# Query and key projections of a linear-attention kernel, one head at a time in the upper and lower 64 rows of the array

## The chip, the cores and the metric

The kernel runs on one core of a Trainium2 chip. The metric is the device time of one execution in microseconds; the time of a version is the median of its runs. TensorE is called PE here, VectorE DVE, ScalarE ACT, GpSimd POOL, and the queue from which transfers are issued SP.

## What is computed

Linear attention with exponential features over 4 batches, 8 heads, 576 tokens and 64 dimensions, then two feed-forward blocks over the 2304 tokens. The part that the change touches is `phi`:

```python
def phi(x):
    proj = np.einsum('bhsd,df->bhsf', x, w_phi)          # w_phi: 64 x 128
    proj = proj - np.max(np.abs(proj), axis=-1, keepdims=True)
    return np.concatenate([np.exp(proj), np.exp(-proj)], axis=-1)
q_p, k_p = (phi(q), phi(k))
kv = np.einsum('bhsf,bhsd->bhfd', k_p, v)
z = np.sum(k_p, axis=2)
num = np.einsum('bhsf,bhfd->bhsd', q_p, kv)
den = np.einsum('bhsf,bhf->bhs', q_p, z)[..., None] + 1e-06
x = num / den
```

The first feed-forward block is 512 to 2048 to 512 with a leaky rectifier; the second has four experts, each 512 to 1024 to 512, whose results are added with the weights of a table of probabilities. All inputs and outputs are float32.

## The kernel before

**Two stages.** The first stage does the attention for 16 pairs of heads (4 batches, 4 pairs each) and, as filler, the first group of four chunks of the first feed-forward block for three blocks of tokens. The second stage is a plain loop over the rest of the feed-forward work (`up` and `down`, lines 211 and 240).

**Precision.** Where float32 products are wanted at the rate of float32r, an operand is split into a rounded part and a rest (names ending in h and l), and three products are added: high by high, high by low, low by high.

**A pair of heads.** The two heads' 64 dimensions lie in the partitions 0 to 63 and 64 to 127 of `kh`, `kl`, `qh`, `ql`. The 576 tokens are cut into four tiles of 128 and one of 64 (`TILES`). `project` (line 339) multiplies a tile of tokens, loaded into the array as weights, by `wbh` and `wbl`: matrices of 128 rows and 256 columns that hold `w_phi` twice, upper left for the one head and lower right for the other, with zeros elsewhere. The result of a tile is 128 tokens by 2 x 128 features in a bank of PSUM. Units of work (`UNITS`, line 36) are two tiles, two tiles, and the tile of 64 tokens: 512, 512 and 256 columns. Per unit DVE finds the largest magnitude of each group of 128 columns (`largest`, line 352, instruction line 355) and subtracts it (`less`, line 358, instruction line 362); for keys ACT takes the exponentials of both signs (`exp_keys`, line 364, instruction line 368). `key_values` (line 372) then adds, per unit, the products of the exponentials with the values (line 379, two heads in two halves of the array's columns) and with ones (line 385, four column quarters). When the three units are through, the sums are copied (`save_kv`), transposed (`turn_kv`, lines 399 and 401) and copied again. For the queries `turn_queries` (line 412) transposes the differences of a head, 256 or 320 tokens at a time (`HALVES`), ACT takes exponentials, and `attend` (line 429) multiplies them by the transposed sums; `invert` and `x_part` divide.

**What sets the order.** The first stage is described as operations with costs per engine, predecessors, a rank and buffers (`op`, line 64). A planner (`Plan.run`, line 69) plays them through and emits each one when its turn comes: of the operations that are ready and have room in their rings it takes the one that can begin first, ties by rank. So the costs that the operations state decide the order of each engine's instructions. Rings limit how far it runs ahead: `bank` has five PSUM banks, which projections, transposes and attention products share; `pmk` two, `pmq` three, `ke` two, `gh` and `gl` five each, `t` two buffers. The operations are named P (project), R (largest), S (less), E (exponentials of keys), KV, CV, TV, T, X, A for attention, W for the words of the first weights, and U, G0, G1, G2, M for the feed-forward filler (PSUM tiles `mm`). A line such as

```python
op(("P", *key), {"t": pe(256, 3) * len(UNITS[u])}, [(n, "l", p)], pr_, alloc=[("bank", key), ("pm" + n, (p, u))],
```

says: PE works for three products of 256 columns per tile, after the split of that tensor, and claims a bank and a buffer for the differences.

Of the kernel before, what the change touches and what calls it, by code (L numbers as in the profile page):

```python
# [11 lines left out]
F32 = mybir.dt.float32  # L12
F32R = mybir.dt.float32r
# [6 lines left out]
P = 128  # L20
B, H, S, D, F = 4, 8, 576, 64, 128
# [5 lines left out]
E, DE = 4, 1024  # L27
# [4 lines left out]
BLK = 512  # L32
BLOCKS = [(t, min(BLK, NT - t)) for t in range(0, NT, BLK)]
NB = len(BLOCKS)
TILES = [(t * P, min(P, S - t * P)) for t in range(-(-S // P))]
UNITS = [(0, 1), (2, 3), (4,)]
HALVES = [(0, 256), (256, 320)]
HMAX = 320
NA = 3
AHEAD = 2  # L40
# [90 lines left out]
def fused(ctx: ExitStack, tc: tile.TileContext, qT, kT, v_main, v_tail, w_phi, alpha, probs, w64, wcat, out):  # L131
    nc = tc.nc
# [145 lines left out]
    with ExitStack() as st1:  # L278
# [8 lines left out]
        for args in (  # L287
            ("kr", 1, F32, P, S), ("qr", 1, F32, P, S), ("v", 1, F32, P, len(TILES), 2, D),
            ("kh", 1, F32R, P, S), ("kl", 1, F32R, P, S), ("qh", 1, F32R, P, S), ("ql", 1, F32R, P, S),
            ("m", 13, F32, P, 4), ("pmk", 2, F32, P, 4, F), ("pmq", 3, F32, P, 4, F), ("ke", 2, F32, P, 4, 2, F),  # L290
            ("kvs", 1, F32, P, 4, F), ("qe", 4, F32, P, 2, HMAX), ("kvt", 4, F32, P, 4, P),
            ("den", 2, F32, P, S), ("dt", 1, F32, P, S), ("num", 2, F32, P, S), ("di", 3, F32, P, S // 32, 1),
            ("gh", 5, F32R, P, BLK), ("gl", 5, F32R, P, BLK), ("t", 2, F32, P, BLK),
        ):
            ring(*args)
        ring("bank", 5, F32, P, 512, space=PSUM)
# [4 lines left out]
        tl = {}  # L301
# [35 lines left out]
                nc.sync.dma_start(new(n + "r", p), (qT if n == "q" else kT)[b, j])  # L337

        def project(p, n, u):
            xh, xl = tl[n + "h", (p,)], tl[n + "l", (p,)]  # L340
            unit = UNITS[u]
            rows = TILES[unit[0]][1]
            ps = new("bank", (n, p, u)).rearrange("p (m f) -> p m f", f=F)
            new("pm" + n, (p, u))
            for i, tile_ in enumerate(unit):
                o = ps[:rows, 2 * i:2 * i + 2, :]
                tok = slice(TILES[tile_][0], TILES[tile_][0] + rows)
                nc.tensor.matmul(o, xh[:, tok], wbh, start=True, stop=False)  # L348
                nc.tensor.matmul(o, xh[:, tok], wbl, start=False, stop=False)  # L349
                nc.tensor.matmul(o, xl[:, tok], wbh, start=False, stop=True)  # L350

        def largest(p, n, u):
            m, rows = 2 * len(UNITS[u]), TILES[UNITS[u][0]][1]
            ps = tl["bank", (n, p, u)].rearrange("p (m f) -> p m f", f=F)
            nc.vector.tensor_reduce(  # L355
                new("m", (n, p, u))[:rows, :m], ps[:rows, :m], AX.X, ALU.max, apply_absolute_value=True)

        def less(p, n, u):
            m, rows = 2 * len(UNITS[u]), TILES[UNITS[u][0]][1]
            ps = tl["bank", (n, p, u)].rearrange("p (m f) -> p m f", f=F)  # L360
            mx = tl["m", (n, p, u)][:rows, :m, None].to_broadcast([rows, m, F])
            nc.vector.tensor_tensor(tl["pm" + n, (p, u)][:rows, :m], ps[:rows, :m], mx, ALU.subtract)  # L362

        def exp_keys(p, u):
            m, rows = 2 * len(UNITS[u]), TILES[UNITS[u][0]][1]
            e = new("ke", (p, u))
            for s, sc in ((0, 1.0), (1, -1.0)):
                nc.scalar.activation(e[:rows, :m, s], tl["pmk", (p, u)][:rows, :m], AF.Exp, scale=sc)

        flat = lambda x: x.rearrange("p i s f -> p i (s f)")  # L370

        def key_values(p, u):

            unit = UNITS[u]
            rows, e, v = TILES[unit[0]][1], flat(tl["ke", (p, u)]), tl["v", p]
            kv = new("kv", p) if u == 0 else tl["kv", p]
            for i, tile_ in enumerate(unit):
                for h in range(2):
                    nc.tensor.matmul(  # L379
                        kv[h * D:(h + 1) * D, 0], v[:rows, tile_, h], e[:rows, 2 * i + h],  # L380
                        start=tile_ == 0, stop=tile_ == len(TILES) - 1, skip_group_check=True)
            for i, tile_ in enumerate(unit):
                for h in range(2):
                    r = 32 * (2 * (tile_ % 2) + h)
                    nc.tensor.matmul(  # L385
                        kv[r:r + 32, 1], ones[:rows], e[:rows, 2 * i + h],
                        start=False, stop=tile_ + 2 >= len(TILES), tile_position=(0, r), skip_group_check=True)

        def save_kv(p, k, e):
            kvs = (new if k == 0 else lambda *x: tl[x])("kvs", p).rearrange("p (k s) f -> p k (s f)", k=2)  # L390
# [21 lines left out]
        def turn_queries(p, h, c):  # L412
            c0, n = HALVES[c]
            ps = new("bank", ("t", p, h, c))
            new("qe", (p, h, c))
            for u, unit in enumerate(UNITS):
                for i, tile_ in enumerate(unit):
                    t0, rows = TILES[tile_]
                    if c0 <= t0 < c0 + n:
                        nc.tensor.transpose(  # L420
                            ps[:, t0 - c0:t0 - c0 + rows], tl["pmq", (p, u)][:rows, 2 * i + h], ident[:rows, :rows])

        def exp_queries(p, h, c):
            n = HALVES[c][1]
# [41 lines left out]
        for p in range(len(pairs)):  # L466
            for n in "kq":
                op(("ld", n, p), {"d": 900}, [], RANK["ld"] + p, alloc=[(n + "r", p)], late=2000,
                   emit=lambda e, p=p, n=n: load(p, n))
                two(n, (p,), n + "r", p, S, [("ld", n, p)], RANK["sp"] + p)  # L470
                for u in range(3):
                    key = (n, p, u)
                    pr_ = RANK["P" + n] + p + 0.1 * u
                    op(("P", *key), {"t": pe(256, 3) * len(UNITS[u])}, [(n, "l", p)], pr_, alloc=[("bank", key), ("pm" + n, (p, u))],
                       behind=[("A", p - AHEAD, 1, 1)] * (p >= AHEAD),
                       reads=[(n + "h", (p,)), (n + "l", (p,))], emit=lambda e, a=(p, n, u): project(*a))
                    op(("R", *key), {"v": dve(N_U[u])}, [("P", *key)], pr_, alloc=[("m", key)],
                       emit=lambda e, a=(p, n, u): largest(*a))
                    op(("S", *key), {"v": dve(N_U[u])}, [("R", *key)], pr_,
                       reads=[("bank", key), ("m", key)], emit=lambda e, a=(p, n, u): less(*a))  # L480
            op(("ld", "v", p), {"d": 900}, [], RANK["ld"] + p, alloc=[("v", p)], late=2000, emit=lambda e, p=p: load(p, "v"))
            for u in range(3):
                op(("E", p, u), {"a": 2 * act(N_U[u])}, [("S", "k", p, u)], RANK["E"] + p + 0.1 * u, alloc=[("ke", (p, u))],
                   reads=[("pmk", (p, u))], emit=lambda e, a=(p, u): exp_keys(*a))
            for u in range(3):
                op(("KV", p, u), {"t": 595 * len(UNITS[u])}, [("E", p, u), ("ld", "v", p)] + [("KV", p, u - 1)] * (u > 0),
                   RANK["KV"] + p + 0.1 * u, alloc=[("kv", p)] if u == 0 else [], reads=[("ke", (p, u)), ("v", p)],
                   emit=lambda e, a=(p, u): key_values(*a))
            for k in range(2):
                op(("CV", p, k), copy_cost(256), [("KV", p, 2)], RANK["TV"] + p, alloc=[("kvs", p)] if k == 0 else [],  # L490
                   behind=[("CV", p, 0)] * k, reads=[("kv", p)], emit=lambda e, a=(p, k): save_kv(*a, e))
            op(("TV", p), {"t": 340}, [("CV", p, 0), ("CV", p, 1)], RANK["TV"] + p, alloc=[("bank", ("kv", p)), ("kvt", p)],
               reads=[("kvs", p)], emit=lambda e, p=p: turn_kv(p))
# [4 lines left out]
            for c in range(2):  # L498
                for h in range(2):
                    key, n = (p, h, c), HALVES[c][1]  # L500
                    pr_ = RANK["Q"] + p + 0.2 * c + 0.1 * h
                    us = ((0,), (1, 2))[c]
                    op(("T", *key), {"t": 110 * len(us) + 110 * (1 - c) + 50 * c}, [("S", "q", p, u) for u in us], pr_,
                       alloc=[("bank", ("t", *key)), ("qe", key)], reads=[("pmq", (p, u)) for u in us], emit=lambda e, a=key: turn_queries(*a))
                    op(("X", *key), {"a": 2 * actp(n)}, [("T", *key)], pr_,
                       reads=[("bank", ("t", *key))], emit=lambda e, a=key: exp_queries(*a))
                    pr_ = RANK["A"] + p + 0.2 * c + 0.1 * h
                    op(("A", *key), {"t": pe(4 * n, 2)}, [("X", *key), *kv_done], pr_, reads=[("qe", key), ("kvt", p)], behind=[("A", p, 0, 0)] * (h + c > 0),
                       alloc=[("bank", ("n", *key))] + [("den", p), ("num", p)] * (h == c == 0),
                       emit=lambda e, a=key: attend(*a))  # L510
                    op(("D", *key), copy_cost(n), [("A", *key)], pr_,
                       reads=[("bank", ("n", *key))], emit=lambda e, a=key: take(*a, "den", e))
                    op(("N", *key), copy_cost(n), [("A", *key)], pr_,
                       reads=[("bank", ("n", *key))], emit=lambda e, a=key: take(*a, "num", e))
# [191 lines left out]
```

## Time and profile before

| | us |
|---|---|
| median of 3 runs | 1438.12 (1437.93 to 1438.18) |
| the profiled execution, device time | 1439.93 |
| its span on the core | 1438.2 |
| PE busy, share of the span | 1418.9, 99% |
| DVE busy | 654.7, 46% |
| ACT busy | 412.4, 29% |
| POOL busy | 212.4, 15% |

The first stage takes roughly the first 300 us. Busy time is the union of the instructions' recorded times; ends of matmuls are modelled, so starts are the better measure, and the distance from one start to the next is called the pace below. PEld is the loading of weights into the array, which overlaps products. A float32 product that is not a transpose appears in the trace as two products and two loads.

### The profile page before, as it was taken

Reading aid. Unit: us, or ns where it says so; the run is one execution under the profiler, and the core shown is the slowest. Engines: PE = TensorE matmul, PEld = TensorE weight load, DVE = VectorE, ACT = ScalarE, POOL = GpSimd, SP = SyncE. Lnnn points to the kernel's source line nnn. Section 1 sums busy time; section 2 is a strip of 40 time slices with the busy share of each in tenths; the row PEclk is TensorE's granted clock in tenths of the full one; section 3 lists DMA queues with packets and bytes.
Section 4 is the critical chain, followed back from the end, with each engine's and each line's share of the span. In section 5 each row is a group of like instructions: output and inputs, shape, how many; then the busy total and the mean of one; then the engine's idle time right before and its main releaser. Section 6 shows DMA issues by size and latency. Waiting matters only on the chain.

```text
span 1438.2 us, 17632 instructions
## 1 busy us (share of the span) xinstructions
PE 1418.9 (99%) x7200; PEld 1152.1 (80%) x7200; DVE 654.7 (46%) x1067; ACT 412.4 (29%) x857; POOL 212.4 (15%) x165
## 2 busy tenths in 40 slices
PE   7999999999999999999999999999999999999998
PEld 4667667778888888888888888888888888888887
DVE  7966656687958855663222222222222222222222
ACT  6877666632212112232021120121210201211110
POOL 3443223102002002011020020020100200200100
PEclk9999999999999999999999999999999999999999
DMA  4311111130202001001020020010100200100001
GB/s 148 112 50 51 50 50 51 53 103 30 88 1 59 30 8 52 1 23 37 0 59 0 1 59 0 8 52 1 30 30 0 59 0 8 52 0 0 30 30 74
DMA packets 25136, 53.67 MB, mean 37 GB/s; under 512 B 3168, under 2 KB 4320, under 8 KB 25056
## 3 DMA queue, kind: packets, MB, share of 16 engines
q1 hardware_dynamic: 25056, 52.55, 12.2%
q8 instruction: 57, 0.93, 0.3%
q14 instruction: 23, 0.19, 0.0%
HBM read 47.82 MB, written 4.72 MB: 37 GB/s over the span
## 4 chain that ended last, share of the span: by engine, by line
PE 94%; DVE 3%; ACT 1%; DMA 1%; issue 0%; SPq 0%; POOL 0%; ACTq 0%; DVEq 0%; POOLq 0%
PE up L208 39%; PE dn L234 39%; PE bank L437 4%; PE kv L379 3%; PE mm L208 2%; PE kv L385 2%; PE mm L234 2%; PE bank L420 1%; PE bank L348 1%; PE bank L349 1%; PE bank L350 1%; DMA st<-w 1%; DMA acc_a<-w 0%; PE bank L401 0%; DVE m L355 0%
## 5 line engine op out<-in xcount | busy, mean ns | idle before, releaser
L208 PE MATMUL up<-Xl,whu 128*128 128x512 f32 (+1 forms) x912 | 334.6, 367 | 0.0
L208 PE MATMUL up<-Xh,whu 128*128 128x512 f32 (+1 forms) x912 | 334.5, 367 | 0.0
L208 PE MATMUL up<-Xh,wlu 128*128 128x512 f32 (+1 forms) x912 | 334.4, 367 | 0.0
L219 ACT ACTIVATE gh<-up 128x512 fp32r<-128x512 f32 (+1 forms) x160 | 88.7, 555 | 539.5 <-PE up L208 539.4
L220 DVE SCALAR_TENSOR_TENSOR gl<-up,gh 128x512 fp32r<-128x512 f32 (+1 forms) x160 | 102.0, 638 | 303.8 <-ACT gh L219 303.7
L234 PE MATMUL dn<-whd,gh 128*128 128x512 f32 x576 | 224.2, 389 | 0.0
L234 PE MATMUL dn<-wld,gh 128*128 128x512 f32 x576 | 224.2, 389 | 0.0
L234 PE MATMUL dn<-whd,gl 128*128 128x512 f32 x576 | 224.1, 389 | 0.0
L208 PEld LDWEIGHTS up<-Xh,whu 128*128 128x128 f32 x912 | 172.0, 189 | 28.6
L208 PEld LDWEIGHTS up<-Xl,whu 128*128 128x128 f32 x912 | 172.0, 189 | 28.4
L208 PEld LDWEIGHTS up<-Xh,wlu 128*128 128x128 f32 x912 | 171.9, 189 | 28.2
L161 POOL TENSOR_TENSOR wlu<-w,whu 128x512 fp32r<-128x512 f32 x44 | 58.2, 1322 | 915.3 <-ACT whu L158 879.7
L234 PEld LDWEIGHTS dn<-whd,gl 128*128 128x128 f32 x576 | 108.1, 188 | 22.5
L234 PEld LDWEIGHTS dn<-whd,gh 128*128 128x128 f32 x576 | 108.2, 188 | 22.1
L234 PEld LDWEIGHTS dn<-wld,gh 128*128 128x128 f32 x576 | 108.2, 188 | 22.1
L271 DVE SCALAR_TENSOR_TENSOR acc_a<-dn,pr,acc_a 128x512 f32<-128x512 f32 x72 | 50.2, 751 | 135.4 <-PE dn L234 135.4
L234 PE MATMUL dn<-gh,wld 128*128 128x512 f32 (+1 forms) x272 | 99.1, 364 | 0.0
L234 PE MATMUL dn<-gh,whd 128*128 128x512 f32 (+1 forms) x272 | 99.1, 364 | 0.0
L234 PE MATMUL dn<-gl,whd 128*128 128x512 f32 (+1 forms) x272 | 99.0, 364 | 0.0
L158 ACT CAST gh<-t 128x512 fp32r<-128x512 f32 (+1 forms) x68 | 38.6, 569 | 134.8 <-DVE t L224 134.6
L437 PE MATMUL bank<-qe,kvt 128*128 128x256 f32 (+1 forms) x256 | 72.6, 417 | 0.9 <-DVE pmk L362 0.9
L158 ACT CAST whu<-w 128x512 fp32r<-128x512 f32 x44 | 27.3, 620 | 136.4 <-PE up L208 121.4
(121 smaller groups left out, 1734.8 us busy)
## 6 DMA issues: line engine op xcount, KB each, us to landing
w<-wcat SPq DMA_DIRECT2D x64, 256.0 KB, 2.6
st<-w SPq DMA_DIRECT2D x24, 512.0 KB, 3.5
kr<-kT SPq DMA_DIRECT2D x16, 288.0 KB, 2.8
qr<-qT SPq DMA_DIRECT2D x16, 288.0 KB, 2.8
out<-o SPq DMA_DIRECT2D x18, 256.0 KB, 2.0
v<-v_main SPq DMA_DIRECT2D x16, 256.0 KB, 3.0
acc_a<-w SPq DMA_DIRECT2D x8, 512.0 KB, 4.5
v<-v_tail SPq DMA_DIRECT2D x16, 32.0 KB, 2.9
```

What stands on the lines that cost most here:

```text
L158: nc.scalar.copy(hi, src)
L161: lo_eng.tensor_tensor(lo, src, f32(hi), ALU.subtract)
L208: nc.tensor.matmul(ps[:, :bn], a[:, cs], x[:, cc, t0:t0 + bn], start=n == 0, stop=n == 3 * CC - 1)
L219: nc.scalar.activation(gh, ps, AF.Relu)
L220: nc.vector.scalar_tensor_tensor(gl, ps, 0.0, f32(gh), ALU.max, ALU.subtract)
L234: nc.tensor.matmul(ps, a, b, start=start and k == 0, stop=stop and k == 2)
L271: nc.vector.scalar_tensor_tensor(av, ps, pe, av, ALU.mult, ALU.add)
L348: nc.tensor.matmul(o, xh[:, tok], wbh, start=True, stop=False)
L349: nc.tensor.matmul(o, xh[:, tok], wbl, start=False, stop=False)
L379: nc.tensor.matmul(kv[h * D:(h + 1) * D, 0], v[:rows, tile_, h], e[:rows, 2 * i + h], start=tile_ == 0, stop=tile_ == len(TILES) - 1, skip ...
L385: nc.tensor.matmul(kv[r:r + 32, 1], ones[:rows], e[:rows, 2 * i + h], start=False, stop=tile_ + 2 >= len(TILES), tile_position=(0, r), ski ...
L437: nc.tensor.matmul(nd[:, :n], tl["kvt", p][:, 2 * h + s], tl["qe", (p, h, c)][:, s, :n], start=s == 0, stop=s == 1)
```

## The change

The units of work become the four full tiles of the first head, the four full tiles of the second head, and the tile of 64 tokens of both. The first two are projected in one operation: for each tile and each of the three terms one product per head, its tokens and `w_phi` from that head's 64 partitions, its 128 columns into that head's own bank. The last tile is projected as before. The maxima, subtractions and exponentials work on units of the same sizes as before, each now of one head. The products of keys and values are emitted for the four full tiles at once, after the exponentials of both heads, and then for the last tile: two operations in place of three. A transpose of the queries' first half waits for its own head's unit alone. The planner is told 12 products of 128 columns as the cost of the 24. The ring of `ke` grows from two to three; `gl` shrinks from five to four and `t` from two to one.

```diff
-UNITS = [(0, 1), (2, 3), (4,)]
+UNITS = [[(0, t) for t in range(4)], [(1, t) for t in range(4)], [(0, 4), (1, 4)]]
+UNIT_OF = {ht: (u, i) for u, unit in enumerate(UNITS) for i, ht in enumerate(unit)}
...
-            ("m", 13, F32, P, 4), ("pmk", 2, F32, P, 4, F), ("pmq", 3, F32, P, 4, F), ("ke", 2, F32, P, 4, 2, F),
+            ("m", 13, F32, P, 4), ("pmk", 2, F32, P, 4, F), ("pmq", 3, F32, P, 4, F), ("ke", 3, F32, P, 4, 2, F),
...
-            ("gh", 5, F32R, P, BLK), ("gl", 5, F32R, P, BLK), ("t", 2, F32, P, BLK),
+            ("gh", 5, F32R, P, BLK), ("gl", 4, F32R, P, BLK), ("t", 1, F32, P, BLK),
...
         def project(p, n, u):
...
-            for i, tile_ in enumerate(unit):
-                o = ps[:rows, 2 * i:2 * i + 2, :]
-                tok = slice(TILES[tile_][0], TILES[tile_][0] + rows)
-                nc.tensor.matmul(o, xh[:, tok], wbh, start=True, stop=False)
-                nc.tensor.matmul(o, xh[:, tok], wbl, start=False, stop=False)
-                nc.tensor.matmul(o, xl[:, tok], wbh, start=False, stop=True)
+            terms = ((xh, wbh), (xh, wbl), (xl, wbh))
+            us = (0, 1) if u == 0 else (2,)
+            ps = [new("bank", (n, p, v)).rearrange("p (m f) -> p m f", f=F) for v in us]
+            for v in us:
+                new("pm" + n, (p, v))
+            if u == 0:
+                for t in range(4):
+                    t0, rows = TILES[t]
+                    for k, (x, w) in enumerate(terms):
+                        for h in range(2):
+                            hs = slice(h * D, (h + 1) * D)
+                            nc.tensor.matmul(ps[h][:rows, t], x[hs, t0:t0 + rows], w[hs, h], start=k == 0, stop=k == 2)
+            else:
+                t0, rows = TILES[4]
+                for k, (x, w) in enumerate(terms):
+                    nc.tensor.matmul(ps[0][:rows, :2], x[:, t0:t0 + rows], w, start=k == 0, stop=k == 2)
...
+        def key_values(p, n):
+
+            ts = range(4) if n == 0 else (4,)
...
+                for u in (0, 2):
+                    key = (n, p, u)
+                    us = (0, 1) if u == 0 else (2,)
+                    op(("P", *key), {"t": pe(128, 12) if u == 0 else pe(256, 3)}, [(n, "l", p)], RANK["P" + n] + p + 0.1 * u,
+                       alloc=[(r, k) for v in us for r, k in (("bank", (n, p, v)), ("pm" + n, (p, v)))],
...
+            for n in range(2):
+                op(("KV", p, n), {"t": 595 * (4, 1)[n]}, [("E", p, u) for u in ((0, 1), (2,))[n]] + [("KV", p, 0) if n else ("ld", "v", p)],
...
-                    us = ((0,), (1, 2))[c]
-                    op(("T", *key), {"t": 110 * len(us) + 110 * (1 - c) + 50 * c}, [("S", "q", p, u) for u in us], pr_,
+                    us = ((h,), (h, 2))[c]
+                    op(("T", *key), {"t": 220 + 50 * c}, [("S", "q", p, u) for u in us], pr_,
```

The order of the instructions moves with it. In the lines below the part after the arrow names what is read and the part before it what is written; the size is that of the result.

On PE, before, the projection of the third pair's keys: its products of 256 columns come in pieces of two tiles, between transposes of the second pair (`pmq` are the queries' differences, `kvs` the sums of keys and values).

```order
L349 MATMUL bank<-wbl,kh 128x256
L350 MATMUL bank<-wbh,kl 128x256
L420 MATMUL bank<-ident,pmq 128x128 x2
L420 MATMUL bank<-ident,pmq 128x64
L399 MATMUL bank<-ident,kvs 128x128 x2
L401 MATMUL bank<-sel,kvs 128x64 x2
L348 MATMUL bank<-wbh,kh 128x256
L349 MATMUL bank<-wbl,kh 128x256
```

The same place in the change:

```order
L413 MATMUL bank<-sel,kvs 128x64 x2
L447 MATMUL bank<-qe,kvt 128x320 x2
L431 MATMUL bank<-ident,pmq 128x128 x2
L431 MATMUL bank<-ident,pmq 128x64
L355 MATMUL bank<-wbh,kh 128x128 x2
L355 MATMUL bank<-wbl,kh 128x128 x2
L355 MATMUL bank<-wbh,kl 128x128 x2
```

Three products of 256 columns have become three times two of 128, and the block of all four tiles stands behind the transposes instead of around them.

On PE, before, the products of keys and values of the second pair (`ke` are the keys' exponentials):

```order
L379 MATMUL kv<-ke,v 64x256 x4
L385 MATMUL kv<-ke,ones 32x256 x4
L420 MATMUL bank<-ident,pmq 128x128 x2
L379 MATMUL kv<-ke,v 64x256 x4
L385 MATMUL kv<-ke,ones 32x256 x4
L348 MATMUL bank<-wbh,kh 64x256
L349 MATMUL bank<-wbl,kh 64x256
```

And in the change:

```order
L359 MATMUL bank<-wbh,ql 64x256
L391 MATMUL kv<-ke,v 64x256 x8
L397 MATMUL kv<-ke,ones 32x256 x8
L447 MATMUL bank<-qe,kvt 128x256 x2
L391 MATMUL kv<-ke,v 64x256 x2
L397 MATMUL kv<-ke,ones 32x256 x2
```

Two blocks of four and four have become one of eight and eight, which stands behind all projections of the pair.

On DVE, before, the first pair's keys, whose exponentials the key products wait for (`acc_a` is the space in which words of weights are put together):

```order
L355 TENSOR_REDUCE m<-bank 128x4
L362 TENSOR_TENSOR pmk<-bank,m 128x512
L168 TENSOR_SCALAR acc_a<-acc_a 128x512
L169 SCALAR_TENSOR_TENSOR acc_a<-acc_a 128x512
L170 TENSOR_SCALAR acc_a<-acc_a 128x512
L171 SCALAR_TENSOR_TENSOR acc_a<-acc_a 128x512
L355 TENSOR_REDUCE m<-bank 128x4 x2
```

And in the change:

```order
L327 TENSOR_TENSOR ql<-qr,qh 128x576
L364 TENSOR_REDUCE m<-bank 128x4 x2
L371 TENSOR_TENSOR pmk<-bank,m 128x512 x2
L364 TENSOR_REDUCE m<-bank 128x4 x2
L371 TENSOR_TENSOR pmq<-bank,m 128x512
```

The maxima and subtractions of two units now follow each other, and the words of the weights come later.

## Rows read from the trace of the kernel before

**Rows 1.** The page: engines' busy time; the chain that ended last, by engine.

```profile
PE 1418.9 (99%) x7200; PEld 1152.1 (80%) x7200; DVE 654.7 (46%) x1067; ACT 412.4 (29%) x857; POOL 212.4 (15%) x165
...
PE 94%; DVE 3%; ACT 1%; DMA 1%; issue 0%; SPq 0%; POOL 0%; ACTq 0%; DVEq 0%; POOLq 0%
```

**Rows 2.** Busy time by stretch: length, PE, PEld, DVE, ACT, POOL, clock, DMA.

```profile
0.00:50.00 50.00, 40.04 (x270) 26.25 (x270) 40.29 (x67) 34.91 (x81) 20.67 (x23) 0.97 0.43 136
50.00:100.00 50.00, 47.12 (x319) 31.98 (x318) 37.69 (x64) 38.66 (x94) 23.22 (x17) 1.00 0.24 75
100.00:250.00 150.00, 150.00 (x1000) 105.50 (x999) 90.68 (x168) 104.48 (x253) 45.30 (x33) 1.00 0.18 52
```

**Rows 3.** Waits of PE over the span: us in total, times, longest us.

```profile
PE kv L379 <- ACT ke L368: 6.0, 6, 2.3
...
PE mm L208 <- DVE t L565: 2.7, 2, 1.7
PE bank L437 <- DVE pmk L362: 0.9, 3, 0.4
PE bank L420 <- DVE pmq L362: 0.8, 1, 0.8
```

**Rows 4.** The chain that ended last, in order of time: start, us, what.

```profile
52.16 0.70 DVE acc_a L171
...
60.85 0.63 ACT ke L368
...
61.52 1.08 PE kv L379 x8
...
93.55 2.75 PE mm L208 x12
```

**Rows 5.** PE in order of time, a projection: start us, us, line, form.

```profile
103.05 0.28 PE L348 MATMUL bank<-wbh,kh 128*128 128x256 f32 x1
...
104.00 0.28 PE L350 MATMUL bank<-wbh,kl 128*128 128x256 f32 x1
```

**Rows 6.** Instructions by line and form: one of the six groups of full projections.

```profile
L348 PE MATMUL bank<-wbh,kh 128*128 128x256 f32 x64 | 22.5, 352 | 4.7 <-ACT wbh L158 4.7
```

**Rows 7.** Loads of weights (PEld) in order of time, at two places.

```profile
102.58 0.19 PEld L348 LDWEIGHTS bank<-wbh,kh 128*128 128x128 f32 x1 [0.41 <-DVE di L450]
102.69 0.19 PEld L349 LDWEIGHTS bank<-wbl,kh 128*128 128x128 f32 x1
...
106.97 0.52 PEld L401 LDWEIGHTS bank<-sel,kvs 128*128 128x128 f32 x4
107.41 0.19 PEld L348 LDWEIGHTS bank<-wbh,qh 128*128 128x128 f32 x1
```

**Rows 8.** Loads by line and form (busy us, mean ns): transposes of 128 and 64 rows.

```profile
L420 PEld LDWEIGHTS bank<-ident,pmq 128*128 128x128 f32 x128 | 15.2, 144 | 9.6 <-issue 3.7 <-POOL wlu L548 1.1 <-DVE pmq L362 0.4
...
L420 PEld LDWEIGHTS bank<-ident,pmq 64*128 64x128 f32 x32 | 4.3, 135 | 5.3 <-issue 5.2 <-DVE acc_a L168 0.2
```

**Rows 9.** PE in order of time: into column tiles and back, and full float32 products.

```profile
108.12 0.28 PE L350 MATMUL bank<-wbh,ql 128*128 128x256 f32 x1
108.33 1.08 PE L379 MATMUL kv<-ke,v 128*64 128x256 f32 x8
109.34 0.64 PE L385 MATMUL kv<-ke,ones 128*32 128x256 f32 x8
109.91 0.33 PE L348 MATMUL bank<-wbh,kh 128*64 128x256 f32 x1
110.08 0.28 PE L349 MATMUL bank<-wbl,kh 128*64 128x256 f32 x1
...
116.13 2.10 PE L437 MATMUL bank<-qe,kvt 128*128 128x256 f32 x8
118.07 0.49 PE L420 MATMUL bank<-ident,pmq 128*128 128x128 f32 x3
```

**Rows 10.** Instructions of DVE and ACT by line and form: busy us, mean ns.

```profile
L355 DVE TENSOR_REDUCE m<-bank 128x4 f32<-128x512 f32 x64 | 41.5, 674 | 2.5 <-PE bank L350 2.3
...
L368 ACT ACTIVATE ke<-pmk 128x512 f32<-128x512 f32 x64 | 36.0, 622 | 1.5 <-DVE pmk L362 1.4
...
L362 DVE TENSOR_TENSOR pmk<-bank,m 128x512 f32<-128x512 f32 x32 | 20.6, 675 | 0.0
```

More of the change, by code (lines that the diff above doesn't have):

```diff
@@ L340, in project @@
             xh, xl = tl[n + "h", (p,)], tl[n + "l", (p,)]
[L341 to L344, printed above, removed]
-            for i, tile_ in enumerate(unit):
-                o = ps[:rows, 2 * i:2 * i + 2, :]
-                tok = slice(TILES[tile_][0], TILES[tile_][0] + rows)
-                nc.tensor.matmul(o, xh[:, tok], wbh, start=True, stop=False)
-                nc.tensor.matmul(o, xh[:, tok], wbl, start=False, stop=False)
-                nc.tensor.matmul(o, xl[:, tok], wbh, start=False, stop=True)
+            terms = ((xh, wbh), (xh, wbl), (xl, wbh))
[14 more added lines that the diff above has]
+                    nc.tensor.matmul(ps[0][:rows, :2], x[:, t0:t0 + rows], w, start=k == 0, stop=k == 2)
         def largest(p, n, u):
-            m, rows = 2 * len(UNITS[u]), TILES[UNITS[u][0]][1]
+            m, rows = len(UNITS[u]), TILES[UNITS[u][0][1]][1]
             ps = tl["bank", (n, p, u)].rearrange("p (m f) -> p m f", f=F)
@@ L358, in less @@
         def less(p, n, u):
-            m, rows = 2 * len(UNITS[u]), TILES[UNITS[u][0]][1]
+            m, rows = len(UNITS[u]), TILES[UNITS[u][0][1]][1]
             ps = tl["bank", (n, p, u)].rearrange("p (m f) -> p m f", f=F)
@@ L364, in exp_keys @@
         def exp_keys(p, u):
-            m, rows = 2 * len(UNITS[u]), TILES[UNITS[u][0]][1]
+            m, rows = len(UNITS[u]), TILES[UNITS[u][0][1]][1]
             e = new("ke", (p, u))
@@ L368, in exp_keys, with keys @@
                 nc.scalar.activation(e[:rows, :m, s], tl["pmk", (p, u)][:rows, :m], AF.Exp, scale=sc)
[L370 to L377, printed above, removed]
+        def key_values(p, n):
+            ts = range(4) if n == 0 else (4,)
+            v = tl["v", p]
+            kv = new("kv", p) if n == 0 else tl["kv", p]
+            def keys(h, t):
+                u, i = UNIT_OF[h, t]
+                return tl["ke", (p, u)].rearrange("p i s f -> p i (s f)")[:TILES[t][1], i]
+            for t in ts:
                 for h in range(2):
                     nc.tensor.matmul(
-                        kv[h * D:(h + 1) * D, 0], v[:rows, tile_, h], e[:rows, 2 * i + h],
-                        start=tile_ == 0, stop=tile_ == len(TILES) - 1, skip_group_check=True)
-            for i, tile_ in enumerate(unit):
+                        kv[h * D:(h + 1) * D, 0], v[:TILES[t][1], t, h], keys(h, t),
+                        start=t == 0, stop=t == len(TILES) - 1, skip_group_check=True)
+            for t in ts:
                 for h in range(2):
-                    r = 32 * (2 * (tile_ % 2) + h)
+                    r = 32 * (2 * (t % 2) + h)
                     nc.tensor.matmul(
-                        kv[r:r + 32, 1], ones[:rows], e[:rows, 2 * i + h],
-                        start=False, stop=tile_ + 2 >= len(TILES), tile_position=(0, r), skip_group_check=True)
+                        kv[r:r + 32, 1], ones[:TILES[t][1]], keys(h, t),
+                        start=False, stop=t + 2 >= len(TILES), tile_position=(0, r), skip_group_check=True)
         def save_kv(p, k, e):
@@ L415, in turn_queries @@
             new("qe", (p, h, c))
[L416 to L421, printed above, removed]
+            for t, (t0, rows) in enumerate(TILES):
+                if c0 <= t0 < c0 + n:
+                    u, i = UNIT_OF[h, t]
+                    nc.tensor.transpose(ps[:, t0 - c0:t0 - c0 + rows], tl["pmq", (p, u)][:rows, i], ident[:rows, :rows])
         def exp_queries(p, h, c):
@@ L470, in fused @@
                 two(n, (p,), n + "r", p, S, [("ld", n, p)], RANK["sp"] + p)
+                for u in (0, 2):
[3 more added lines that the diff above has]
+                       alloc=[(r, k) for v in us for r, k in (("bank", (n, p, v)), ("pm" + n, (p, v)))],
+                       behind=[("A", p - AHEAD, 1, 1)] * (p >= AHEAD),
+                       reads=[(n + "h", (p,)), (n + "l", (p,))], emit=lambda e, a=(p, n, u): project(*a))
                 for u in range(3):
@@ L473, in fused @@
                     pr_ = RANK["P" + n] + p + 0.1 * u
[L474 to L477, printed above, removed]
+                    op(("R", *key), {"v": dve(N_U[u])}, [("P", n, p, u - u % 2)], pr_, alloc=[("m", key)],
                        emit=lambda e, a=(p, n, u): largest(*a))
@@ L484, in fused @@
                    reads=[("pmk", (p, u))], emit=lambda e, a=(p, u): exp_keys(*a))
[L485 to L488, printed above, removed]
+            for n in range(2):
+                op(("KV", p, n), {"t": 595 * (4, 1)[n]}, [("E", p, u) for u in ((0, 1), (2,))[n]] + [("KV", p, 0) if n else ("ld", "v", p)],
+                   RANK["KV"] + p + 0.1 * n, alloc=[("kv", p)] if n == 0 else [],
+                   reads=[("v", p)] + [("ke", (p, u)) for u in ((0, 1), (2,))[n]], emit=lambda e, a=(p, n): key_values(*a))
             for k in range(2):
-                op(("CV", p, k), copy_cost(256), [("KV", p, 2)], RANK["TV"] + p, alloc=[("kvs", p)] if k == 0 else [],
+                op(("CV", p, k), copy_cost(256), [("KV", p, 1)], RANK["TV"] + p, alloc=[("kvs", p)] if k == 0 else [],
                    behind=[("CV", p, 0)] * k, reads=[("kv", p)], emit=lambda e, a=(p, k): save_kv(*a, e))
```

## Prediction

> **What bounds the kernel now.** I read the page first: TensorE (PE) is busy 99% of the span, and the chain of work that ended last lies 94% on PE [rows 1]. So PE's time is the kernel's time, unless a stretch shows otherwise. The table by stretch of time shows where it does: PE is idle for 9.96 us in the first 50 us, for 2.88 in the next 50, and not at all from 100 to 250 us [rows 2]; the granted clock is full there. The list of waits says for what: six waits of the key products (kv) for the exponentials of the keys (ke), 6.0 us in all, and small ones for VectorE (DVE) [rows 3]. Last the chain in order of time: at 52 us it still runs through DVE's words of the feed-forward weights and ScalarE's exponentials, and it turns to PE only at 61.5 us, with the kv product that had waited for ke [rows 4]. The reader should see two regimes: in the first 60 us a microsecond saved on PE becomes a wait, behind that it counts in full, and new waits count everywhere.
>
> **What the change does to the projections.** Per pair of heads and tensor, four tiles of 128 tokens each took three products over 256 columns: 384 in all (six groups like the one row shown, 64 each [rows 6]), and eight follow each other in 0.95 us, 0.119 us each [rows 5]. They become 384 couples: one product in the upper 64 rows of the array, one in the lower, 128 columns each. At the 0.119 us of 256 columns, 128 would stream in half of that, 0.06 us.
>
> But each of the 768 products loads its own tokens as weights, 128 columns of them, where one load served both heads. Two views price a load. After a pause, where nothing hides it, the second load starts 0.11 us behind the first; and where the products are only 64 columns long, four loads take 0.44 us, again 0.11 each [rows 7]. Half the rows do not halve it: the transposes' loads are recorded at 144 ns with 128 rows, at 135 ns with 64 [rows 8]. So if the two loads of a couple run side by side, the couple is bound by its loads, at 0.11 us, not by its columns: 384 × (0.119 − 0.11) = 3.5 us saved instead of 22.7.
>
> Do they run side by side? No row of the kernel before has two products in different rows of the array. In different columns it has: eight kv products of 256 columns start within 1.01 us, while eight full ones of the same length take 1.94 [rows 9], so two column halves work at once, loads included. I take the same for rows. The bounds of a couple are 0.06 us (columns alone) and 0.22 us (two loads in turn); I take 0.11, between them, since it is the load that rows 7 measure.
>
> The Trainium skill says otherwise of the gain: in "TensorE: Matmul & The Clock Gate", Part 3, products packed in different row groups take about the time of one of them plus some 4 ns for each further one. By that a couple would cost one short product, and this term would be −22.7 us instead of −3.5. The page's own rule on loads, that their time goes by columns and not by rows (Part 2), pulls the other way; rows 7 and 8 agree with it.
>
> **Changes of the array's shape.** Going from a full product to a column-tiled one takes 0.21 us from start to start instead of 0.12, and the first product behind a change is late by its load: 0.17 instead of 0.12 for 64 columns [rows 9]. That is 0.09 and 0.05 to 0.11, about 0.15 us for a change of shape. Along PE's order I count 202 changes before (products of float32r taken as using all columns, since rows 9 show no step between 128- and 64-column ones of them) and 187 in the change: the kv block of each pair is entered twice instead of three times, and the row-tiled blocks are entered 15 times from another shape, the others standing behind a 64-row transpose. 15 fewer × 0.15 = −2.2 us; the 15 entries load 128 columns uncovered, 0.05 more each, +0.8. Sum −1.4 us, between −2.2 and +2.
>
> **New waits.** Maxima, subtractions and exponentials stay the same in number and size (4 × 128 columns per unit, as before), so DVE and ScalarE do no more work. What moves is when a kv block may start. It now takes four tiles of both heads, so both first units must be through. From the end of the projections that is two maxima and two subtractions in a row on DVE, 4 × 0.675 us, then two exponentials, 2 × 0.62: 3.9 us. Before, the first half could start after one unit: 2.6 us [rows 10]. The release comes 1.35 us later. Where PE has other work it costs nothing: from 100 to 250 us PE never ran dry, and the cover there (the queries' projections, transposes, products of the feed-forward part, 2.75 us per twelve [rows 4]) stands in the new order too. Between the second pair's key projections and its kv block I count some 3.5 to 4 us of PE work, hardly the 3.9 that is needed, and DVE is 80% busy then. So I charge each of the six places that wait today with the full 1.35: **+8.1 us**. The lower bound is 0 (the cover suffices), the upper 16 × 1.35 = 21.6.
>
> Claiming two of five banks and two subtraction buffers at once can hold back the block until DVE has read both. Waits for DVE at the banks are 0.9 and 0.8 us today [rows 3]; I take half of their sum, +0.9, between 0 and 3.4. The third ke buffer removes a claim that no wait shows: 0. One t buffer instead of two, and four gl instead of five: the wait of the up products for t is 2.7 us in two places today [rows 3]; in the new order mostly twelve or twenty-four products stand together, so DVE's chain has room: 0, and another 2.7 if that cover is gone. The loads of the queue (DMA) are the same in number and size and swap a few places; no wait of PE is for one [rows 3]: 0.
>
> **Sum.** −3.5 − 1.4 + 8.1 + 0.9 = +4.1 us. The profiled execution took 1439.9 us (span 1438.2), so it would take 1444.0. The median of the timed runs is 1.8 lower, 1438.1: **1442.2 us**. With the bounds of the terms this case reaches from 1435 to 1452.
>
> **Rivals.**
> A, the couples cost half (0.06 us): what the page on TensorE says. For it: column halves do overlap. Against: rows 7, a load of 0.11 us. Then 22.7 us come off PE, but not for the first four pairs of sixteen, whose end DVE and ScalarE set [rows 4]: −17.0; with −1.4 for shapes and +8.1 for waits −10.3: 1427.8. Chance 0.15. It decides if a couple takes under 0.09 us.
> B, the halves do not work at once, or the shorter products run at a lower rate: a couple takes 0.22 us. For it: rows 9 show overlap for columns only, and for other operands; unrounded float32 products take 0.24 us for 256 columns in each of two passes [rows 9], and at that rate 128 columns also take 0.24 us a couple. Against: the two halves read different partitions. 384 × 0.101 = +38.8, −1.4, and PE so slow that it covers the waits: 1475.5; at 0.24 us 1483. Chance 0.20.
> C, the other side of my sign with the same couples: the planner's order gives enough cover, PE waits no longer than today. It decides if 3.9 us of PE work stand between a pair's key projections and its kv block in the first 100 us. Then −3.5 − 1.4: 1433.2. Chance 0.13.
> My case keeps 0.52.
>
> **How the numbers follow.** 0.2%, 2.9 us, is about what a measurement of this kernel tells from no change: from 1435.2 to 1441.0. Faster: A, 0.15, and 0.09 of C: 0.24. Same: the rest of C, 0.04, and the part of my case in which the waits come to under 7 us, 0.14: 0.18. Slower: B and 0.38 of my case: 0.58. As both signs hold much of the chance, the range must take in A and the nearer half of B: 1426 to 1478; my case alone is 1435 to 1452.
>
> **What would show it.** In the profile after, couples should start 0.11 us apart, with the two products of a couple some nanoseconds apart, and loads back to back at 0.11. PE's idle time in the first 100 us should grow from 12.8 to about 22 us, with waits for ScalarE's copies and exponentials and for DVE; from 100 to 250 us it should stay near 0. A couple at 0.06 or at 0.22 us proves A or B; idle time of 13 us or less in the first 100 us proves C. I would be wrong altogether if the time went to the later part of the run, behind 310 us, which the change does not touch.

## The result, and the profile after

**1449.1 us** (median of 4 runs, 1448.4 to 1451.1) against 1438.1 (1437.9 to 1438.2): ratio 1.0079, 95% interval 1.0061 to 1.0096. Slower by 11.0 us, as forecast in sign and inside the range of 1426 to 1478, but 6.9 us more than the 4.1 of the sum. The profiled execution took 1449.07 us, its span 1447.3.

Busy time of the changed kernel by stretch: length, PE, PEld, DVE, ACT, POOL, granted clock, DMA share, GB/s.

```profile
0.00:50.00 50.00, 41.87 (x301) 29.87 (x303) 40.16 (x63) 31.27 (x72) 18.25 (x21) 0.93 0.45 136
50.00:100.00 50.00, 45.50 (x363) 29.69 (x363) 35.23 (x60) 33.08 (x84) 18.91 (x14) 0.90 0.23 69
100.00:250.00 150.00, 149.47 (x1131) 107.34 (x1128) 87.60 (x156) 97.98 (x238) 43.18 (x31) 1.00 0.17 49
```

Against [rows 2], PE is as busy in the first 100 us as before (87.4 and 87.2 us), ScalarE less (64.4 and 73.6), and the granted clock is 0.93 and 0.90 where it was 0.97 and 1.00. So PE is not idle for longer (12.6 us of the first 100, 12.8 before); part of its busy time is the same work at 1.2 GHz. In the trace's clock record the low stretches of the first 100 us are 41.6 to 48.5, 65.5 to 69.0 and 82.6 to 89.4 us, 17.1 us in all; before there is one, 12.3 to 15.7. Also, the record begins with full clock at 17.8 us instead of 8.8; ahead of that couples stand 0.21 us apart, twice their later distance. PE in order of time, at 8 us and at 97 us (start, us, line, form):

```profile
7.93 0.41 PE L355 MATMUL bank<-wbh,qh 64*128 64x128 f32 x2
8.14 0.41 PE L355 MATMUL bank<-wbl,qh 64*128 64x128 f32 x2
8.36 0.41 PE L355 MATMUL bank<-wbh,ql 64*128 64x128 f32 x2
```

```profile
96.67 0.19 PEld L355 LDWEIGHTS bank<-wbh,kh 64*128 64x128 f32 x2 [0.44 <-issue]
96.67 0.33 PE L355 MATMUL bank<-wbh,kh 64*128 64x128 f32 x2
96.78 0.19 PEld L355 LDWEIGHTS bank<-wbl,kh 64*128 64x128 f32 x2
...
96.83 0.28 PE L355 MATMUL bank<-wbl,kh 64*128 64x128 f32 x2
96.89 0.19 PEld L355 LDWEIGHTS bank<-wbh,kl 64*128 64x128 f32 x2
...
96.95 0.28 PE L355 MATMUL bank<-wbh,kl 64*128 64x128 f32 x2
97.00 0.19 PEld L355 LDWEIGHTS bank<-wbh,kh 64*128 64x128 f32 x2
97.06 0.28 PE L355 MATMUL bank<-wbh,kh 64*128 64x128 f32 x2
```

The second shows what was forecast: both halves of a couple in one row, loads and couples 0.11 us apart. In this block the halves start 3 to 6 ns apart, as in 204 of the 384 couples; in most others the second half starts some 0.06 us (99 couples) or 0.11 us (42) behind the first, and the couples follow each other at the same pace. Waits of PE over the span, against [rows 3]:

```profile
PE bank L447 <- DVE pmk L371: 3.4, 3, 1.5
PE bank L447 <- ACT kvt L138: 1.7, 1, 1.7
PE bank L411 <- ACT kvs L138: 1.7, 2, 1.2
PE kv L391 <- ACT ke L377: 0.9, 3, 0.4
```

The wait of the kv block for its exponentials, on which I put +8.1 us, has fallen from 6.0 to 0.9 us.

**Where the time went.** A mark splits the run: the start of the last of the 80 attention products of the first five pairs, with 12 up products before it in every kernel here. The rows that it lies in, and the ones behind, before and after:

```profile
98.21 2.31 PE L437 MATMUL bank<-qe,kvt 128*128 128x320 f32 x8
100.36 0.38 PE L420 MATMUL bank<-ident,pmq 128*128 128x128 f32 x2
```

```profile
113.09 1.34 PE L447 MATMUL bank<-qe,kvt 128*128 128x320 f32 x4
114.36 0.33 PE L355 MATMUL bank<-wbh,kh 64*128 64x128 f32 x2
```

The mark stands at 100.1 us before and at 114.0 after: **13.9 us are lost ahead of it, and 4.8 won back behind it** (span less mark: 1338.1 and 1333.3). Some 2.4 us on either side are moved work: in the change one more small block of keys and values, one more set of the sums' transposes and three more transposes of queries stand ahead of the mark, in the kernel before behind it. So some 11.5 us are lost on the same work. Counted by the work that PE has been given, at the full-clock paces of the kernel before (an estimate), the change is level with it at 35 us, 5.7 us behind at 50, 7.2 at 75, and 11.5 from 90 us to the mark.

### The profile page after: what moved, and what is told of

It is laid out like the page before. It is cut to its first block, busy times and chain, and to the rows that moved or that the text cites. A ratio compares the mean times of both kernels' runs of the same rounds, so it can differ in the third digit from the quotient of the medians.

```text
span 1447.3 us, 18421 instructions
## 1 busy us (share of the span) xinstructions
PE 1428.6 (99%) x7584; PEld 1161.3 (80%) x7584; DVE 658.6 (46%) x1066; ACT 412.6 (29%) x860; POOL 210.6 (15%) x163
## 4 chain that ended last, share of the span: by engine, by line
PE 91%; DVE 5%; ACT 2%; DMA 1%; issue 1%; POOL 0%; SPq 0%; DVEq 0%; ACTq 0%; POOLq 0%
PE dn L236 37%; PE up L210 37%; PE bank L447 4%; PE bank L355 3%; PE kv L391 3%; PE mm L210 2%; PE mm L236 2%; PE kv L397 2%; PE bank L431 1%; DMA st<-w 1%; PE bank L359 1%; DVE u L172 0%; ACT qe L437 0%; DVE t L225 0%; DVE m L364 0%
```

## The experiments

The mark, what follows it, and the clock's record in each profile (low: us at 1.2 GHz between the first full-clock record and the mark). A profile is one execution, and executions of one kernel differ by up to 5.3 us (e7: 1445.8 to 1451.2).

| kernel | median, us | ratio (95%) | mark | span − mark | full clock from | low |
|---|---|---|---|---|---|---|
| before | 1438.1 | | 100.1 | 1338.1 | 8.8 | 3.4 |
| the change | 1449.1 | 1.0079 (1.0061–1.0096) | 114.0 | 1333.3 | 17.8 | 17.1 |
| e1 told cost | 1450.2 | 1.0075 (1.0059–1.0091) | 110.6 | 1337.1 | 19.5 | 13.7 |
| e2 rings | 1438.7 | 1.0001 (0.9992–1.0011) | 99.6 | 1338.1 | 9.3 | 3.4 |
| e4 kv merged | 1438.8 | 1.0002 (0.9993–1.0012) | 103.5 | 1334.0 | 10.3 | 10.2 |
| e5 merged, full products | 1438.7 | 1.0001 (0.9991–1.0010) | 101.4 | 1334.2 | 11.4 | 0 |
| e6 couples late | 1442.9 | 1.0028 (1.0018–1.0037) | 103.4 | 1337.5 | 11.3 | 3.4 |
| e7 couples early | 1448.7 | 1.0067 (1.0045–1.0089) | 114.3 | 1331.5 | 17.9 | 13.6 |
| e10 no rows | 1443.7 | 1.0041 (1.0026–1.0056) | 111.4 | 1330.6 | 17.2 | 10.2 |
| e11 filler | 1453.0 | 1.0102 (1.0085–1.0118) | 118.0 | 1332.9 | 19.8 | 3.4 |
| e12 warm change | 1449.0 | 1.0066 (1.0054–1.0079) | 112.8 | 1333.2 | 17.2 | 10.2 |
| e13 warm before | 1438.6 | 1.0001 (0.9992–1.0010) | 99.3 | 1337.9 | 4.7 | 3.4 |

My first theory was the plan: it is told 676 ns for a block of couples that takes twice as long.

**e1, the told cost.**

```diff
-{"t": pe(128, 12) if u == 0 else pe(256, 3)}
+{"t": 1400 if u == 0 else pe(256, 3)}
```

> The changed kernel, with one number altered: the plan is told 1400 ns for a block of 24 couples, the length that the trace shows (1.29 us start to start and the drains), and not 676. Plan theory (the plan sets the order for a block that it takes for half as long, TensorE then stands in pieces of the first 90 us and its granted clock falls): most of the loss goes, 1438 to 1443 us, with less than 8 us at 1.2 GHz where the change has 17. Tile theory (the couples, the drains and the blocks of keys and values that need both units cost what is lost, whatever the plan is told): 1447 to 1451 us, as the change.

1450.2 us. The plan theory falls; the order changes and the loss stays: the mark comes 3.4 us earlier than in the change, and 3.8 more pass behind it, where the clock is low once more (309.6 to 313.0 us).

**e2, the rings alone, in the kernel before.**

```diff
-("ke", 2, ...), ("gl", 5, ...), ("t", 2, ...)
+("ke", 3, ...), ("gl", 4, ...), ("t", 1, ...)
```

> The kernel before with the change's rings alone: ke 3, gl 4, t 1. Plan theory and tile theory: 1438 us within 1 us, since the up steps wait for no t. Ring theory (the one t buffer holds the up steps of the first 300 us back): 1441 us or more, with new waits of products for t or gl.

1438.7: the rings cost nothing.

**e4, one kv block for both units, in the kernel before with the change's rings.**

```diff
-for u in range(3): op(("KV", p, u), {"t": 595 * len(UNITS[u])}, [("E", p, u), ...
+for n in range(2): op(("KV", p, n), {"t": 595 * (4, 1)[n]}, [("E", p, u) for u in ((0, 1), (2,))[n]] + ...
```

> The kernel before with the change's rings and with the two blocks of keys and values merged into one that needs both exponentials. By the sum of the prediction the merged block is released 1.35 us later at six places, up to +8: 1441 to 1446 us. Plan theory: the plan knows this wait and puts other work in it, 1437 to 1441 us. Tile theory says nothing of it, as no couple is in it.

1438.8. The mark comes 3.4 us later, with the same work ahead of it, and 4.1 us are won behind it. My largest term is thereby refuted as a cost: in sum the merged block costs nothing. The gain is in the blocks themselves. Two blocks took 1.58 us each (108.33 to 109.91 in [rows 9]); the one that takes their place needs 2.88, and one entry of 0.2 to 0.3 us goes:

```profile
130.80 1.95 PE L383 MATMUL kv<-ke,v 128*64 128x256 f32 x16
132.68 1.07 PE L389 MATMUL kv<-ke,ones 128*32 128x256 f32 x16
133.68 0.44 PE L424 MATMUL bank<-ident,pmq 128*128 128x128 f32 x2
```

Behind the mark the kv blocks with their entries take 47.0 us in e4 and 51.2 before: **0.42 us for each of the ten blocks that go**.

**e5, the projections of two units in one block too, of full products.**

```diff
+for v in us:
+    for i, tile_ in enumerate(UNITS[v]):
...
+        o = ps[v][:rows, 2 * i:2 * i + 2, :]
+        for k, (x, w) in enumerate(terms):
+            nc.tensor.matmul(o, x[:, t0:t0 + rows], w, start=k == 0, stop=k == 2)
```

> As the run with merged keys and values, and the projections of two units are one block as well, of twelve full products of 256 columns, that claims two banks at once; the plan is told 676 ns for it, as in the change (the trace gives 1.43). No couple, no row-tiled product. Plan theory: most of the change's loss is here, 1444 to 1451 us, with the granted clock at 1.2 GHz for 10 us or more of the first 90. Tile theory: 1441 us or less, with the clock as before (3.4 us at 1.2 GHz).

1438.7, granted clock full from 11.4 us on, although the plan is told the wrong cost. What is left is what e4 and e5 lack: units by head, and couples, whose products have 128 columns instead of 256.

**e6 and e7, couples in a part of the pairs** (units by tile and the full products of e5 in the others, with the change's plan).

```diff
+TILED = lambda p: p >= 6      # e6; p < 6 in e7
```

> The changed kernel, but its first six pairs of heads (k and q, 12 of the 32 blocks; those of the first 100 us) are projected by full products of 256 columns into two banks by tile; couples from the seventh pair on. Clock theory (couples cost and save nothing by themselves, but in the first 90 us, where TensorE also stands, they leave it too little work and the granted clock falls): 1435 to 1440 us, 10 us or less at 1.2 GHz. Couple theory (each couple block costs some 0.3 us more than its trace shows, by drains and moved work, wherever it stands): 20 of 32 blocks keep 7 of the 11 us, about 1445 us.

> The reverse: couples in the first six pairs of heads, full products of 256 columns from the seventh on. Clock theory: the whole loss stays, 1445 to 1451 us, with 13 us or more at 1.2 GHz. Couple theory: 12 of 32 blocks, +4, about 1442 us.

1442.9 and 1448.7. The early pairs hold nearly the whole loss (e7: mark 114.3, as in the change), but late couples are not free either. e5 and e6 issue PE's groups of products in the same order, so they can be laid side by side. PE in order of time where attention products are followed by a projection, in e5 and in e6:

```profile
100.48 1.34 PE L442 MATMUL bank<-qe,kvt 128*128 128x320 f32 x4
101.42 0.52 PE L351 MATMUL bank<-wbh,kh 128*128 128x256 f32 x1
```

```profile
102.46 1.34 PE L457 MATMUL bank<-qe,kvt 128*128 128x320 f32 x4
103.74 0.33 PE L365 MATMUL bank<-wbh,kh 64*128 64x128 f32 x2
```

From the first of the four attention products to the projection it is 0.94 us in e5 and 1.27 in e6. At all seven places of this kind behind 100 us the difference is the same: **0.33 us for each entry**. A full product starts with the attention product still running, a couple does not. The block itself is 0.17 shorter, and the second product behind it 0.06 later, so 0.22 us are lost at each of the seven; the five blocks behind transposes of 64 rows gain slightly. In all, e6 needs 3.3 us more than e5 behind the mark: 2.5 in its twenty blocks, and 0.8 at a kv block at 174 us, which now waits for its exponentials.

**e8 and e9, one block twelve times over**, at 150 us where PE never idles: couples in the change, full products in the control.

```diff
+for r in range(12 if (p, n) == (8, "k") else 1):
```

> The changed kernel with one block of 24 couples' products issued 12 times over: the keys of the ninth pair, at about 150 us, where TensorE never idles before or after. 11 more times 12 couples. At the 0.117 us of the trace: 15.4 us more, 0.117 us for each further couple. If the couples count as less work for the clock even where TensorE never stands, the granted clock falls to 1.2 GHz inside this stretch or right behind it, and the couples inside take about 0.23 us; if only idle time lets it fall, it stays full there.

> The control: all blocks by full products of 256 columns into two banks, and the same block (keys of the ninth pair) issued 12 times over: 11 times 12 products more. At the pace of 0.119 us: 15.7 us more, and the granted clock stays full there under either theory.

One execution each: 1465.2 and 1452.7 us. Two of the stretches, first of e8 (94 products of couples in 5 us), then of e9:

```profile
155.00:160.00 5.00, 5.00 (x94) 5.00 (x94) 0.00 (x0) 0.00 (x0) 1.00 (x1) 1.00 0.00 0
160.00:165.00 5.00, 5.00 (x94) 5.00 (x94) 0.00 (x0) 0.00 (x0) 0.00 (x0) 1.00 0.02 3
```

```profile
150.00:155.00 5.00, 5.00 (x45) 5.00 (x44) 0.00 (x0) 0.00 (x0) 0.00 (x0) 1.00 0.01 3
155.00:160.00 5.00, 5.00 (x45) 5.00 (x44) 0.00 (x0) 0.00 (x0) 0.00 (x0) 1.00 0.00 0
```

The repeated block takes 1.340 us for 12 couples and 1.420 for 12 full products: 0.1117 and 0.1183 each. And the clock stays full through 16 us of nothing but couples: couples alone do not let it fall.

**e10, no rows**: the change's order, 12 full products of 128 columns for a block.

```diff
-for k, (x, w) in enumerate(terms):
-    for h in range(2):
-        hs = slice(h * D, (h + 1) * D)
-        nc.tensor.matmul(ps[h][:rows, t], x[hs, t0:t0 + rows], w[hs, h], start=k == 0, stop=k == 2)
+for h, x, w, a, z in ((0, xh, wbh, 1, 0), (0, xh, wbl, 0, 1), (1, xh, wbh, 1, 1)):
+    nc.tensor.matmul(ps[h][:rows, t], x[:, t0:t0 + rows], w[:, h], start=a == 1, stop=z == 1)
```

> The changed kernel in its own order, with every block of 24 couples' products replaced by 12 products of the full array and 128 columns (one head's columns of the matrix, whose other rows are zero), one per couple. Left out: the product of the inputs' low half, and for the second head that of the matrix's low half. A full product of 128 columns is bound by the same load, 0.112 us, so a block takes as long as with couples; what goes is the division into rows: the 0.33 us that a block behind an attention product lost in the run with late couples, and half the rows standing empty. Row theory (the changes of shape, and couples that leave TensorE too little work in the first 90 us so that the clock falls): 1437 to 1441 us, 7 us or less at 1.2 GHz. Order theory (the order in which head-wise units put the work is what lets TensorE stand and the clock fall; rows cost only the entries): 1443 to 1447 us, with 13 us or more at 1.2 GHz.

1443.7, and 10.2 us low: between the two. Without rows 2.7 us are won ahead of the mark and 2.7 behind it (the seven entries of 0.33 there are gone). But the mark still stands at 111.4, so **most of the early loss is there without a single couple**, though not without products of 128 columns. The clock falls there too.

**e11, filler**: more PE work in the first five pairs.

```diff
+for _ in range(6 if p < 5 else 0):
+    nc.tensor.matmul(ps[0][:, :2], xh[:, :P], wbh, start=True, stop=True)
```

> The changed kernel with six further full products of 256 columns, whose result is overwritten, ahead of each block of couples of the first five pairs of heads: 60 products, 7.1 us of TensorE work at full clock in the first 90 us. If the low clock costs what its share of the loss seems (some 8 of the 11 us), and further work of TensorE keeps it up: 7 us or less at 1.2 GHz, and 1443 to 1449 us, no slower than the change in spite of the work added. If the clock falls all the same, or its fall costs nothing: 1453 to 1457 us.

1453.0: the clock of the first case, the time of the second (1453 to 1457). Low time falls from 17.1 to 3.4 us; the mark comes 4.0 us later. Busy time by stretch:

```profile
0.00:50.00 50.00, 43.03 (x331) 31.18 (x331) 36.14 (x58) 28.52 (x65) 16.57 (x20) 1.00 0.41 130
50.00:100.00 50.00, 43.34 (x341) 29.11 (x340) 35.86 (x59) 34.02 (x85) 20.06 (x15) 0.97 0.24 75
```

In the second half the clock is 0.97 instead of 0.90, and PE is busy for 2.2 us less: much of what the clock gives back, PE spends standing. Were all 60 products on the path (7.1 us at full clock), 13.7 us of low clock cost 3.1 us; a rough reading, since some of the 60 lay in idle time and the first twelve ran at 1.2 GHz.

**e12 and e13, eight products ahead**, in the 5 us in which PE stands at the start; change and before.

```diff
+z = Xh[:, 0, :BLK]
+nc.vector.memset(f32(z), 0.0)
...
+for _ in range(8):
+    nc.tensor.matmul(warm_ps, z[:, :P], z, start=True, stop=True)
```

> The changed kernel with eight further full products of 512 zero columns that wait for nothing but a fill with zeros, in the 5 us that TensorE stands at the program's start; order and all else as in the change, where the granted clock is full only from 17.8 us on (8.8 in the kernel before). If the late rise is part of the loss: full clock from 12 us or earlier, and 1443 to 1447 us. If it costs nothing, since VectorE and ScalarE set the end of the first stage: 1448 to 1451 us even so.

> The kernel before with the same eight products ahead. Full clock before 8.8 us and no fall at 12.3: 1434 to 1437 us, if the clock at the start sets the end of the stage; 1437 to 1439 us if VectorE and ScalarE set it.

1449.0 and 1438.6: nothing in either. In the change the full clock still comes at 17.2 us; in the kernel before it comes at 4.7 instead of 8.8, falls at 11.6 all the same, and moves the mark by 0.8 us. e12 has PE's order of the change and lacks the last of its three low stretches, 6.8 us (the others are 6.8 and 3.4). At 82 us it is 0.6 us behind the change, at 90 us 1.2 ahead of it: 1.8 us for 6.8, so low clock costs 0.26 us per us there, and 13.7 us of it 3.6. The repeated runs of a kernel, of which each lists its mean clock, give about the same: over eleven kernels the span grows by 0.26 us with each us at 1.2 GHz. This is rough: it is 0.15 in e12's five runs and 0.63 in e7's four, and the clock is listed to 0.001, which is 2.9 us of low clock.

No kernel tried beats the one before.

## Why the prediction was right in sign, and short in size

- **Products (−3.5): right mechanism, size −2.5.** A couple takes 0.1117 us, a full product of 256 columns 0.1183: 384 × 0.0066. e10's full products of 128 columns follow each other at 0.112 us too, so neither rows nor columns set the pace; what is left is the load, which no run takes away. Rivals A (0.06) and B (0.22) fall. The Trainium skill, "TensorE: Matmul & The Clock Gate", Part 3, has packed products some 4 ns apart and a pack about as long as one product. The trace agrees on the second, if the one product is priced with its load, 0.112 us as in e10, and not at the 0.06 of its columns, as I did for rival A; on the first it agrees in 204 couples of 384.
- **Shape (−1.4): mis-sized in both parts.** I priced every change at 0.15 us and an entry to couples 0.05 higher. The entry behind attention costs 0.33 (e6; the same in e10, where it is gone), 0.22 with what the block gains, so e6 lost by couples behind the mark where I expected a gain. The other way, a kv block that goes is worth 0.42 us (e4), by which sixteen are worth 6.7 and not 2.2.
- **Waits (+8.1): this step failed.** I counted PE's work between a pair's key projections and its kv block in the old order, and charged six places. The new order puts other work in between: the wait shrank to 0.9, and e4, with this edit and the rings alone, is no slower. PE's idle time in the first 100 us did not grow to the 22 that I forecast; it is 12.6. Without this term the sum is −4.0, faster, so **the sign came right by luck**: the loss lies where the sum has no term. The range, 52 us wide, tells little.
- **Rival C: its condition came true, its time did not.** I had said that idle time of 13 us or less proves C. PE's waits are indeed no longer than before, yet the time is 1449.1 and not 1433.2: idle time does not show work that runs at 1.2 GHz. The 1435 to 1452 of my own case were too narrow for its terms, whose bounds add up to −5.7 and +26.2, or 1432 to 1464.
- **Two banks (+0.9) and rings (0): nothing** in the time (e5, e2), though PE's waits for DVE at the banks are 4.0 us in the change and were 1.7.
- **What I had not seen** is the first stage. With units by head in the early pairs the fifth pair is through 10 to 14 us later (the change, e1, e7, e10), without them 3.4 later at most (e2, e4, e5, e6). Told cost, rings, merged kv blocks, two banks and rows are excluded as its main cause by e1, e2, e4, e5 and e10. But the same four kernels project these pairs by products of 128 columns, so that no run tells the one from the other. The clock is a part: 13.7 us more at 1.2 GHz, by e11 and e12 3.1 to 3.6 us (6.9 if PE had set the pace throughout). The late full clock at the start is none: at 35 us the change is still level with the kernel before. Rows give 2.7, which overlaps with the clock, as e10 has 6.8 us less of low time.
- **What stays open** is what makes up the rest, some 5 to 8 of the 11.5 us. A reading that no run tests: a unit of one head releases the transposes of that head only; those of the second head wait for the second unit's maximum and subtraction, where a unit of two tiles released both. ScalarE's waits in the first 115 us were what suggested it. In the change:

```profile
ACT qe L437 <- PE bank L431: 8.0, 5, 2.9
...
ACT den L138 <- PE bank L447: 4.7, 7, 3.0
```

Before, the waits for a transpose (L420) are 0.6 us. But in e5, whose mark is early, they are 4.7, and of the 8.0 in the change 4.3 lie ahead of 23 us, where it is not yet behind. So these rows do not carry the reading.

The balance of the two profiles is +13.9 to the mark and −4.8 behind it; +9.1 in the spans and +11.0 in the medians, as the profiled execution of before lay 1.8 above its median. Behind the mark the moved work gives −2.4, the merged kv blocks −4.2 (e4), and the couples take +2.5 (e6), together −4.1 of the −4.8. The test "wrong if the time goes behind 310 us" held: it goes to the first 114.

## What to carry to other kernels

Dividing the array saves little (6% a product here) where each half still needs its own load and the load is as long as the product: compare loads first, then the price of entering the shape from what stands ahead of it (0.33 us here against 0.17 gained in a block). A regrouping that only renames which tiles form a unit also changes when the next step may start; try it without the new instructions (e10 does it in part) before putting the loss down to them. And where a first stage runs on chains over three engines, look at the clock and the order together: removing 13.7 us of low clock gave back some 3 us (e11). Equal idle time does not mean equal time where the granted clock differs, and a merged block is priced by its own rows, not by the wait ahead of it alone.

## What the hardware showed unexpectedly

- Full clock survived 16 us of pure couples (e8). At the start the change stayed at 1.2 GHz through its first couples: from 5.0 to 12.2 us it issues projections with a single pause of 0.06 us, and the full clock is recorded from 17.8 us; e10 with its 128-column products is the same (17.2). With full products of 256 columns e5 has it from 11.4 and the kernel before from 8.8.
- The eight products ahead brought the full clock at 4.7 us in e13 and at 17.2 in e12; so they alone do not decide it.
- Ahead of each fall of the clock in the change PE had stood: two waits of 0.5 and 0.8 us ahead of 41.6 us, one of 1.7 ahead of 65.5, one of 1.2 ahead of 82.6 and one of 1.4 around it. Such a wait does not always bring a fall: e5 has waits of 1.2, 1.3 and 1.0 us in its first 100 us and keeps the full clock.
